# The first block fetch placed ahead of the third chunk's transposes, and a separate tile for VectorE's discarded squares

## The chip, the cores and the metric

The kernel runs on one core of a Trainium2 chip. Five engines take part: TensorE (PE; its weight loads are listed as PEld), VectorE (DVE), ScalarE (ACT), GpSimd (POOL) and SyncE (SP, which here only issues DMAs). The metric is device time of one execution in microseconds, the median over repeated runs.

## What is computed

The input x has 8 sequences of 3584 tokens with 192 features, so 28672 tokens. A causal filter of 7 taps comes first, one set of taps for each of 8 groups of 24 features; each token of the result then goes to one of 8 experts. Cut to what matters:

```python
w = softmax(weight, axis=-1)                       # 8 heads x 7 taps
x = einsum('hk,bskhg->bshg', w, windows_of(x_pad)) # causal filter
xn = x / (norm(x) + 1e-6);  en = emb / (norm(emb) + 1e-6)
logits = xn @ en.T / tau
e = argmax(logits);  gate = softmax(logits)[e]
out = gate * (relu(x @ w1[e]) @ w2[e])             # 192 -> 1024 -> 192
```

## The kernel before

The tokens are handled in 16 **chunks** of 1792 (112 partitions x 16 columns). Matrix products run on pairs of fp16 values, a rounded part and a remainder, so each weight and each token row exists twice.

**The start.** `run()` first loads and prepares the weights of the 8 experts, e = 0 to 7, through three staging buffers. `prep_weights` sums squares on PE (L318) and takes the diagonal of that sum on DVE (L323, whose full result `w_dg` is thrown away and only its row sum kept); ACT then writes the rounded halves (L337, three instructions an expert) and DVE the remainders (L341, three an expert). Between these steps `dispatch` hands out steps of the chunks: `mix` (filter on PE L413, copy on ACT L418, squares of the 16 columns, 12 on ACT L425 and 4 on DVE L428, all of whose full results go to a tile `sq` and are thrown away) and `route` (scaling L457, cast L459, remainder L461 and L464 into `rows`, logits L496, softmax and rank up to L570, which writes `di`, the place of each token in its expert's list; then POOL scatters the rows to `rows_d` in memory, L601). The first two chunks are transposed by PE; from the third on, 16 transposing DMAs a chunk (`turn`, L597) do it, issued by SP.

**Blocks.** Once two chunks are counted, `hand_out` calls `select` (L632), about 25 small DVE instructions in tiles named `sl_*`, each with one buffer in the pool `lone`. They end with two casts (L676, L677) that write `sel`: expert and starting row of each block. The first hand-out makes 7 blocks of 256 tokens. `fetch` (L711) has SP read `sel`, then issue a transposing load `e_xT` (L721) and a small load `e_mt` (L724), which wait for the scatters of the two chunks. `expert` copies the expert's weights to `slot` (L703, L706) and runs a block: 40 matmuls `h_ps` (L776), relu on ACT and DVE (L780, L782), 48 matmuls `o_ps` (L799), gate on ACT (L804), scatter of results by POOL (L806). Blocks and the later chunks' steps are then interleaved to the end of the program.

**What sets the order.** SP runs in the order of the program text. The other engines' instructions are put in an order by a scheduler that works on estimated times and on which tile is free; once placed, each engine runs its list in order. A tile of a pool with one buffer can be handed out again only when its last user is done, so two users of one tag keep the order of the program text between them. `PRE` is (14, 8): after the weights, 14 steps of the chunks, then 8, then the interleaved loop. Before, the hand-out and three fetches stand after the first of the two rounds:

Of the kernel before, what the change touches and what calls it, by code (L numbers as in the profile page):

```python
# [13 lines left out]
F32 = mybir.dt.float32  # L14
# [11 lines left out]
D = 192  # L26
# [3 lines left out]
TP = 112  # L30
# [37 lines left out]
def _dep(tc, frm, to, sync=True):  # L68
    cls = mybir.DependencyClass.Sync if sync else mybir.DependencyClass.NoSync
    tc.add_manual_dep(  # L70
        frm, to, mybir.DependencyInfo(cls, mybir.DependencyReason.DATA),
        reason="routed rows are written before they are read",
    )


class _Moe:
# [217 lines left out]
    def prep_weights(self, e, st):  # L294
        nc = self.nc
        img = self.res[:, e * RES:(e + 1) * RES]


        st, sw = st
        sr, sv = (v.bitcast(BF16).rearrange("p (n k) -> p n k", k=2)[:, :, 1]  # L300
                  for v in (st, sw))
        acc = self.sp.tile([128, 2], F32, tag="w_acc", name="w_acc")
        for k, cols in enumerate(
                ([(sr, 128, i) for i in range(NFC)]
                 + [(sr, 64, i) for i in range(NFC, 2 * NFC)],
                 [(sv, 128, i) for i in range(NFC * D // 128)])):
            if k and e >= BEHIND:

                i = nc.scalar.activation(
                    out=img[:, W2:W2 + NFC * D], in_=sw, func=AF.Square,  # L310
                    accum_out=acc[:, k:k + 1]).ins
                _dep(self.tc, i, self.act[1].name, False)
                yield
                continue
            tr = self.ps("h", [128, 128], F32, "tr_ps")
            for n, (v, rows, i) in enumerate(cols):
                v = v[0:rows, i * 128:(i + 1) * 128]
                i = nc.tensor.matmul(out=tr, lhsT=v, rhs=v, start=(n == 0),  # L318
                                     stop=(n == len(cols) - 1)).ins
                if e >= BEHIND:  # L320
                    _dep(self.tc, i, self.turned.name, False)
            dg = self.sp.tile([128, D], F32, tag="sq", name="w_dg")[:, 0:128]
            nc.vector.scalar_tensor_tensor(  # L323
                out=dg, in0=tr, scalar=1.0, in1=self.idf, op0=ALU.mult,
                op1=ALU.mult, accum_out=acc[:, k:k + 1])
            yield
        ps = self.ps("h", [128, 2], F32, "n2_ps")
        nc.tensor.matmul(out=ps, lhsT=self.onef, rhs=acc, start=True, stop=True)
        s, si = self.pow2(ps, [128, 2], 198, "w_p")
        s1, s2 = s[:, 0:1], s[:, 1:2]  # L330
        nc.vector.tensor_tensor(out=img[:, WS:WS + 2].bitcast(F32), in0=si[:, 0:1],
                                in1=si[:, 1:2], op=ALU.mult)
        yield
        xb = img[:, 2 * F:W2]
        b = img[:, W2:WS].rearrange("p (c d) -> p c d", d=2 * D)
        s_b = sw.rearrange("p (c d) -> p c d", d=D)
        hi = [nc.scalar.activation(out=o, in_=i, func=AF.Copy, scale=m).ins  # L337
              for o, i, m in ((img[:, 0:F], st[:, 0:F], s1),
                              (xb[0:64, :], st[0:64, F:2 * F], s1[0:64]),
                              (b[:, :, 0:D], s_b, s2))]  # L340
        lo = [nc.vector.scalar_tensor_tensor(  # L341
            out=o, in0=i, scalar=m, in1=h, op0=ALU.mult, op1=ALU.subtract).ins
              for o, i, m, h in (
                  (img[:, F:2 * F], st[:, 0:F], s1, img[:, 0:F]),
                  (xb[64:128, :], st[0:64, F:2 * F], s1[0:64], xb[0:64, :]),
                  (b[:, :, D:], s_b, s2, b[:, :, 0:D]))]
        if e >= BEHIND - 1:
            for i in hi:
                _dep(self.tc, i, self.act[e >= BEHIND].name, False)
        for i in lo:  # L350
            if e >= BEHIND - 2:
                _dep(self.tc, i, self.dve[e >= BEHIND].name, False)
            elif e:
                _dep(self.tc, i, self.cut.name, False)
        yield


    def load_x(self, c):
# [46 lines left out]
    def mix(self, c, ring, first):  # L405
        nc, sp = self.nc, self.sp

        yield _Gate(self.asked[c] + LAND_X)
        xt = self.xts[c]
        xc = xt[0:TP]  # L410
        for h in range(H):
            ps = self.ps(ring, [TP, NT, G], F32, "conv_ps")
            i = nc.tensor.matmul(out=ps, lhsT=self.band[:, h, :],  # L413
                                 rhs=xt[:, :, h * G:(h + 1) * G],
                                 start=True, stop=True).ins
            self.behind(i)
            self.clk += STEPC
            nc.scalar.copy(out=xc[:, :, h * G:(h + 1) * G], in_=ps)  # L418
            yield 0.0, 0.46

        n2 = sp.tile([TP, NT], F32, tag="n2", name="n2")
        for t in range(NT):
            sq = sp.tile([128, D], F32, tag="sq", name="sq")[0:TP, :]
            if t % 4 < NACT:
                nc.scalar.activation(out=sq, in_=xc[:, t, :], func=AF.Square,  # L425
                                     accum_out=n2[:, t:t + 1])
            else:
                nc.vector.scalar_tensor_tensor(  # L428
                    out=sq, in0=xc[:, t, :], scalar=1.0, in1=xc[:, t, :],
                    op0=ALU.mult, op1=ALU.mult, accum_out=n2[:, t:t + 1])  # L430
            if t % 2:
                yield ((0.54, 0.0), (0.27, 0.35), (0.0, 0.7))[
                    (t % 4 < NACT) + ((t - 1) % 4 < NACT)]
        s, si = self.pow2(n2[:], [TP, NT], 195, "x_p")
        y = self.rsqrt(n2[:], [TP, NT], "x_r")
        f = sp.tile([TP, NT], F32, tag="f", name="f")
        nc.vector.tensor_tensor(out=f, in0=n2, in1=y, op=ALU.mult)
        nc.vector.scalar_tensor_tensor(out=f, in0=f, scalar=1e-6, in1=s,
                                       op0=ALU.add, op1=ALU.mult)
        nc.vector.reciprocal(out=f, in_=f)  # L440
        nc.vector.tensor_scalar(out=f, in0=f, scalar1=self.rtau[:, 0:1],
                                scalar2=None, op0=ALU.mult)

        yield 1.5, 0.0
        self.mixed[c] = xc, s, si, f
# [460 lines left out]
    def run(self):  # L906
# [15 lines left out]
        first = min(PICK)  # L922
        a, spent = self.dispatch(first, "h"), [0.0, 0.0]
        for e in range(E):
# [9 lines left out]
            if e == BEHIND - 1:  # L934
                for _ in a:
                    pass
                a = self.dispatch(first, "r")
        self.weights_in = True
        for n in PRE:
            for _ in range(n):  # L940
                spent = [s + t for s, t in zip(spent, next(a))]
            if not self.subs:
                self.hand_out(first)
                while self.ready < min(3, len(self.subs)):
                    self.fetch()
        self.gated = True
        live, due, done, out = next(a, None), [0.0, 0.0], False, 0.0
        while live or self.pend or not done or self.at < len(self.subs):
            if self.at < len(self.subs):
                for v in self.expert():  # L950
                    self.steer(spent)
                    out = min(1.0, out + self.pace)
# [41 lines left out]
```

## Time and profile before

| | |
|---|---|
| median of 3 runs | 1357.72 us (1354.47 to 1360.31) |
| the profiled execution | 1352.22 us |
| its span in the trace | 1350.1 us |
| PE busy | 1188.8 us (88%) |
| DVE, ACT, POOL busy | 835.1, 583.3, 543.7 us |
| chain that ended last, largest shares | issue 25%; POOL `out_dram` L806 7% |

The profiled execution is 2.1 us longer than its span and 5.5 us shorter than the median. The page cuts the span in 40 slices and gives each engine's busy tenths:

```profile
PE   5673789897889998999888999889999999999998
DVE  3967657667776756676676564635445555467475
PEclk9666789999899998999998999989999999999999
```

A slice is 33.8 us; the change lies in slices 2 to 6 (34 to 203 us). In a timeline a row is one run of like instructions: start, time until the last ends, engine, line, what it writes and reads, how many (x8), and in brackets how long the engine was idle before it and which event ended that. "issue" or "remote" there means that the trace shows no event.

### The profile page before, as it was taken

The numbers are of one execution on the slowest core, as the hardware profiler recorded it, in microseconds if no ns is written. First come the engines' busy times: TensorE is split into PE (matmuls) and PEld (weight loads), VectorE is DVE, ScalarE is ACT, GpSimd is POOL, SyncE is SP. The second block draws the span as 40 slices with busy tenths as digits, with TensorE's granted clock in tenths as the row PEclk, the third lists the DMA queues.
The fourth block names the chain that finished last, engine by engine and source line by source line (L and its number), as shares of the span: only waits on it lengthen the run. The fifth ranks groups of instructions, "written<-read, shape, count | busy, mean of one in ns | idle before, by whom it ended". The sixth has DMA issues, their size and how long they took to land. (4 is left out here: it accounts for less than half of the span.)

```text
span 1350.1 us, 28933 instructions
## 1 busy us (share of the span) xinstructions
PE 1188.8 (88%) x10572; PEld 911.7 (68%) x10572; DVE 835.1 (62%) x2207; ACT 583.3 (43%) x1343; POOL 543.7 (40%) x541
## 2 busy tenths in 40 slices
PE   5673789897889998999888999889999999999998
PEld 3542578686776676767556667567777777799787
DVE  3967657667776756676676564635445555467475
ACT  4957344444534544544444533324333333333332
POOL 0064252455444546456445555663222222223232
PEclk9666789999899998999998999989999999999999
DMA  9473534536357444565446344312212121113120
GB/s 262 125 221 91 118 76 105 129 94 132 97 128 147 98 115 106 124 138 130 117 119 145 83 103 84 97 63 57 51 37 52 42 52 43 36 40 66 33 45 22
DMA packets 273950, 129.10 MB, mean 96 GB/s; under 512 B 215774, under 2 KB 264285, under 8 KB 273808
## 3 DMA queue, kind: packets, MB, share of 16 engines
q1 hardware_dynamic: 250000, 80.39, 28.2%
q0 software_dynamic: 23808, 46.87, 11.8%
q8 instruction: 83, 1.36, 0.4%
q14 instruction: 59, 0.48, 0.1%
HBM read 38.35 MB, written 47.53 MB: 64 GB/s over the span
## 5 line engine op out<-in xcount | busy, mean ns | idle before, releaser
L799 PE MATMUL o_ps<-slot,hid 128*128 128x192 f16 x5544 | 516.8, 250 | 68.4 <-issue 39.8
L799 PEld LDWEIGHTS <-hid 128*128 128x128 f16 x5544 | 467.4, 100 | 118.7 <-issue 65.8
L776 PE MATMUL h_ps<-e_xT,slot 128*128 128x256 f16 (+2 forms) x2944 | 502.3, 304 | 13.0 <-issue 8.2
L806 POOL DMA_INDIRECT out_dram<-y,e_mt x231 | 259.2, 1122 | 510.4 <-ACT y L804 464.6
L776 PEld LDWEIGHTS <-slot 128*128 128x128 f16 x3680 | 326.5, 99 | 202.4 <-issue 31.2
L782 DVE SCALAR_TENSOR_TENSOR hid<-h_ps,hid 128x512 f16<-128x512 f32 x462 | 309.6, 687 | 194.5 <-ACT hid L780 152.6
L780 ACT ACTIVATE hid<-h_ps 128x512 f16<-128x512 f32 x462 | 267.1, 598 | 236.3 <-PE h_ps L776 166.1
L601 POOL DMA_INDIRECT rows_d<-rows,di x256 | 266.9, 1042 | 222.6 <-issue 84.0
L804 ACT ACTIVATE y<-o_ps,g 128x192 f32<-128x192 f32 x231 | 95.4, 420 | 337.7 <-PE o_ps L799 260.8
L776 PE MATMUL h_ps<-e_xf,slot 128*128 128x256 f16 (+2 forms) x736 | 211.3, 303 | 2.0 <-issue 2.0
L706 DVE COPY slot<-res 128x3074 f16 x88 | 85.9, 976 | 162.4 <-PE o_ps L799 103.3
L413 PE MATMUL conv_ps<-xt,band 128*112 128x384 f32 x256 | 112.2, 545 | 19.0 <-ACT xt L418 7.9
L418 ACT COPY xt<-conv_ps 112x384 f32<-112x384 f32 x128 | 60.1, 480 | 73.9 <-PE conv_ps L413 54.1
L459 ACT CAST rows<-xt 112x768 f16<-112x768 f32 x64 | 52.9, 830 | 75.7 <-DMA rows_d<-rows,di 35.0
L703 DVE COPY slot<-res 128x3072 f16 x88 | 83.7, 952 | 0.0
L496 PEld LDWEIGHTS <-xT 128*112 128x112 f16 x768 | 58.7, 149 | 33.7 <-DMA xT<-rows 20.8
L496 PE MATMUL lg_ps<-ma,xT 128*112 128x16 f16 x512 | 57.9, 204 | 21.3 <-DMA xT<-rows 19.1
L413 PEld LDWEIGHTS conv_ps<-xt,band 128*112 128x112 f32 x256 | 43.2, 195 | 41.1 <-issue 20.5
L461 DVE TENSOR_TENSOR rows<-xt,rows 112x512 f16<-112x512 f32 x64 | 44.0, 687 | 40.5 <-ACT rows L459 30.9
L425 ACT ACTIVATE sq<-xt 112x192 f32<-112x192 f32 x192 | 67.8, 356 | 2.7 <-DVE sq L428 1.7
L457 DVE TENSOR_TENSOR xt<-xt,x_p_s 112x768 f32<-112x768 f32 x64 | 58.3, 952 | 0.2
L496 PE MATMUL lg_ps<-mb,xT 128*112 128x16 f16 x256 | 47.2, 206 | 1.9 <-ACT xT L492 1.4
(163 smaller groups left out, 528.7 us busy)
## 6 DMA issues: line engine op xcount, KB each, us to landing
xt<-in_dram SPq DMA_DIRECT2D x39, 384.0 KB
xt<-in_dram SPq DMA_DIRECT2D x3, 1440.0 KB
rows_d<-rows,di POOLq DMA_INDIRECT x256
res<-in_dram SPq DMA_DIRECT2D x5, 768.0 KB
out_dram<-y,e_mt POOLq DMA_INDIRECT x231
xT<-rows SPq DMA_TRANSPOSE x224
xt<-in_dram SPq DMA_DIRECT2D x2, 1536.0 KB
hid<-in_dram SPq DMA_DIRECT2D x3, 768.0 KB
```

The source lines that it names most:

```text
L413: i = nc.tensor.matmul(out=ps, lhsT=self.band[:, h, :], rhs=xt[:, :, h * G:(h + 1) * G], start=True, stop=True).ins
L425: nc.scalar.activation(out=sq, in_=xc[:, t, :], func=AF.Square, accum_out=n2[:, t:t + 1])
L496: i = nc.tensor.matmul(out=lg[:, g * GX + a, :], lhsT=xT[:, a, k, :], rhs=self.mb if k == 1 else self.ma, start=(k == 0), stop=(k == 2)).ins
L601: i = self.nc.gpsimd.indirect_dma_start(out=self.rows_d[:, :], out_offset=bass.IndirectOffsetOnAxis(ap=idx, axis=0), in_=src, in_offset=No ...
L703: self.under(nc.vector.tensor_copy(out=self.slot[:, 0:W2], in_=v).ins)
L706: self.nc.vector.tensor_copy(out=self.slot[:, W2:], in_=self.res[:, bass.ds(self.we + W2, RES - W2)])
L776: self.mm = nc.tensor.matmul(out=ps[:, c, :], lhsT=w1(o, b + c), rhs=xk[k], start=(i == 0), stop=(i == 4)).ins
L780: self.step = nc.scalar.activation(out=hh[:, b:b + m, :], in_=ps, func=AF.Relu).ins
L782: self.low = nc.vector.scalar_tensor_tensor(out=hl[:, b:b + m, :], in0=ps, scalar=0.0, in1=hh[:, b:b + m, :], op0=ALU.max, op1=ALU.subtrac ...
L799: self.mm = nc.tensor.matmul(out=o, lhsT=h[:, c, q], rhs=w2[:, c, k:k + D], start=(c + i == 0), stop=(c == NFC - 1 and i == 2)).ins
L804: self.step = nc.scalar.activation(out=y, in_=o, func=AF.Copy, scale=g[:, a:a + 1]).ins
L806: i = nc.gpsimd.indirect_dma_start(out=self.out[:, :], out_offset=bass.IndirectOffsetOnAxis(ap=mt[:, a, 0:1], axis=0), in_=y, in_offset=No ...
```

## The change

Two edits. The first hand-out moves from behind the first 14 steps to ahead of them, and each of the two rounds of `PRE` begins with one fetch, where three fetches stood together; the third fetch then comes from `expert`. The thrown-away results of VectorE (four squares a chunk, and `w_dg`) go to a tile of their own, `waste`, in the one-buffer pool under the tag `sl_ge`, a tag that `select` also uses; ScalarE's squares keep `sq`. Lines below L358 move down by 4, those below L425 by 5.

```diff
@@ prep_weights
-            dg = self.sp.tile([128, D], F32, tag="sq", name="w_dg")[:, 0:128]
+            dg = self.waste(128, 128)
@@ new
+    def waste(self, p, n):
+        return self.lp.tile([128, D], F32, tag="sl_ge", name="waste")[0:p, 0:n]
@@ mix
         for t in range(NT):
-            sq = sp.tile([128, D], F32, tag="sq", name="sq")[0:TP, :]
             if t % 4 < NACT:
+                sq = sp.tile([128, D], F32, tag="sq", name="sq")[0:TP, :]
                 nc.scalar.activation(out=sq, ...)
             else:
                 nc.vector.scalar_tensor_tensor(
-                    out=sq, in0=xc[:, t, :], scalar=1.0, in1=xc[:, t, :],
+                    out=self.waste(TP, D), in0=xc[:, t, :], scalar=1.0,
+                    in1=xc[:, t, :],
@@ run
         self.weights_in = True
+        self.hand_out(first)
         for n in PRE:
+            if self.ready < len(self.subs):
+                self.fetch()
             for _ in range(n):
                 spent = [s + t for s, t in zip(spent, next(a))]
-            if not self.subs:
-                self.hand_out(first)
-                while self.ready < min(3, len(self.subs)):
-                    self.fetch()
         self.gated = True
```

On SP, after the last load of weights (`hid`), before: the 16 turns of the third chunk in two groups of eight (`rows_96`), with the input of the fifth chunk (`xt`) between, then the first fetch.

```order
L289 DMA hid<-in_dram 128x8x192
L597 DMA_TRANSPOSE xT<-rows_96 128x3x112 x8
L366 DMA xt<-in_dram 112x192
L375 DMA xt<-in_dram 128x15x192
L597 DMA_TRANSPOSE xT<-rows_96 128x3x112 x8
L714 TENSOR_LOAD sel_3584_1419
L714 ISA x2
L721 ISA
L721 DMA_TRANSPOSE e_xT<-rows_d 128x3x256
L724 ISA
L724 DMA e_mt<-rows_d 128x2x2
```
After:

```order
L289 DMA hid<-in_dram 128x8x192
L719 TENSOR_LOAD sel_3584_1294
L719 ISA x2
L726 ISA
L726 DMA_TRANSPOSE e_xT<-rows_d 128x3x256
L729 ISA
L729 DMA e_mt<-rows_d 128x2x2
L602 DMA_TRANSPOSE xT<-rows_96 128x3x112 x8
L370 DMA xt<-in_dram 112x192
L379 DMA xt<-in_dram 128x15x192
L602 DMA_TRANSPOSE xT<-rows_96 128x3x112 x8
```
The first fetch's six rows, with its reading of `sel`, now stand ahead of the 16 turns and the load of `xt`; the second fetch stands where the first stood, and the rest of SP's list keeps its order.

On DVE, before, the place where `sel` is written: L341 is the last remainder of expert 5's weights, `n_1070` the squares of the third chunk.

```order
L341 SCALAR_TENSOR_TENSOR res<-res,w_p_s 128x8x192
L683 TENSOR_TENSOR sl_t<-sl_t,sl_av 1x8
L663 TENSOR_REDUCE sl_ro<-sl_df 1x7
L676 CAST sel_3584_1419<-sl_se 1x7
L428 SCALAR_TENSOR_TENSOR sq,n_1070<-xt 112x192
L684 SCALAR_TENSOR_TENSOR start<-sl_t,start 1x8
L664 SCALAR_TENSOR_TENSOR sl_ro<-jf,sl_ro 1x7
L677 CAST sel_3584_1419<-sl_ro 1x7
```
After, with the remainders of expert 7 (`hid` is its staging buffer) and the `sl_ge` memset that opens the part of `select` behind the tag:

```order
L341 SCALAR_TENSOR_TENSOR res<-hid,w_p_s,res 128x1024
L658 MEMSET sl_ge 1x63
L341 SCALAR_TENSOR_TENSOR res<-hid,w_p_s,res 64x1024
L143 SCALAR_TENSOR_TENSOR x_r_t<-x_r_t,n_1070 112x16
L659 TENSOR_TENSOR sl_ge<-sl_a,jf 1x7x8
L341 SCALAR_TENSOR_TENSOR res<-hid,w_p_s,res 128x8x192
```
And ten rows further on, where the casts to `sel` now stand (`n_1224` belongs to the fourth chunk):

```order
L681 CAST sel_3584_1294<-sl_se 1x7
L153 TENSOR_SCALAR x_p_e<-n_1224 112x16
L134 TENSOR_SCALAR x_r_sh<-n_1224 112x16
L145 SCALAR_TENSOR_TENSOR x_r_y<-x_r_t,x_r_y 112x16
L669 SCALAR_TENSOR_TENSOR sl_ro<-jf,sl_ro 1x7
L442 TENSOR_TENSOR f<-n_1070,x_r_y 112x16
L682 CAST sel_3584_1294<-sl_ro 1x7
```
The memset stood at the start of the program before, and `sel` was complete ahead of expert 6's remainders. Now the memset comes behind the third of the four squares of the fourth chunk, and the casts come behind the remainders of experts 6 and 7 and behind the third chunk's scaling and rows.

ScalarE's list changes at the start too: expert 1's three L337 stood behind the first chunk's casts (L459) and now stand ahead of them; those of experts 6 and 7 now stand ahead of the casts of the third and the fourth chunk.

On PE, before, the last logits of the third chunk and the start of block 1:

```order
L496 MATMUL lg_ps<-ma,xT 112x16
L496 LDWEIGHTS xT
L496 MATMUL lg_ps<-mb,xT 112x16
L496 LDWEIGHTS xT
L496 MATMUL lg_ps<-ma,xT 112x16
L776 LDWEIGHTS slot
L776 MATMUL h_ps<-e_xT,slot 128x256
```
After, a place inside block 1's first products:

```order
L781 LDWEIGHTS slot
L781 MATMUL h_ps<-e_xT,slot 128x256
L781 LDWEIGHTS slot
L781 MATMUL h_ps<-e_xT,slot 128x256
L501 LDWEIGHTS xT
L501 MATMUL lg_ps<-ma,xT 112x16
L501 LDWEIGHTS xT
L501 MATMUL lg_ps<-mb,xT 112x16
L501 LDWEIGHTS xT
L501 MATMUL lg_ps<-ma,xT 112x16
L781 LDWEIGHTS slot
```
Before, all 48 logits of the third chunk precede block 1. Now they are spread between its products, in groups of three to nine, and the last stand behind most of block 1 and ahead of block 2.

## Rows read from the trace of the kernel before

**Rows 1.** Busy us (instructions) by stretch: PE, PEld, DVE, ACT, POOL; granted clock; DMA; GB/s

```profile
125.00:150.00 25.00, 10.43 (x55) 7.36 (x56) 20.31 (x54) 12.22 (x24) 0.00 (x0) 0.50 0.52 116
150.00:175.00 25.00, 17.95 (x162) 14.88 (x161) 14.95 (x60) 5.93 (x11) 10.07 (x10) 0.84 0.53 114
900.00:1100.00 200.00, 195.94 (x1744) 145.54 (x1744) 96.22 (x164) 71.70 (x138) 54.90 (x54) 0.98 0.22 49
```

**Rows 2.** PE groups, 85 to 250 us: busy, mean ns | idle before, releasers

```profile
L799 PE MATMUL o_ps<-slot,hid 128*128 128x192 f16 x401 | 40.7, 257 | 9.8 <-issue 7.0 <-DVE hid L782 2.4 <-DVE slot L706 0.3
...
L496 PE MATMUL lg_ps<-ma,xT 128*112 128x16 f16 x72 | 9.9, 216 | 16.8 <-DMA xT<-rows 16.8
```

**Rows 3.** PE timeline: start, duration, work xcount [idle before <-releaser]

```profile
122.62 0.26 PE L496 MATMUL lg_ps<-ma,xT 128*112 128x16 f16 x1 [9.52 <-DMA xT<-rows]
...
149.11 3.31 PE L776 MATMUL h_ps<-e_xT,slot 128*128 128x256 f16 x16 [2.51 <-DMA e_xT<-rows_d]
...
158.89 0.82 PE L776 MATMUL h_ps<-e_xT,slot 128*128 128x256 f16 x6
...
163.25 2.33 PE L799 MATMUL o_ps<-slot,hid 128*128 128x192 f16 x24
...
177.08 1.06 PE L776 MATMUL h_ps<-e_xT,slot 128*128 128x256 f16 x4
```

**Rows 4.** Timeline of SP's DMA queue: start, time to issue, transfer

```profile
120.09 11.18 SPq L597 DMA_TRANSPOSE xT<-rows  x8
...
132.49 12.07 SPq L597 DMA_TRANSPOSE xT<-rows  x8
146.06 1.23 SPq L721 DMA_TRANSPOSE e_xT<-rows_d  x1
...
148.70 1.24 SPq L721 DMA_TRANSPOSE e_xT<-rows_d  x1
...
153.34 10.88 SPq L597 DMA_TRANSPOSE xT<-rows  x8
```

**Rows 5.** DVE timeline, from the second chunk's `di` to the last weights

```profile
93.14 0.15 DVE L570 TENSOR_SCALAR di<-dr 112x16 int32<-112x16 f32 x1
...
93.50 1.28 DVE L341 SCALAR_TENSOR_TENSOR res<-hid,w_p_s,res 128x1024 f16<-128x1024 f32 x1
...
96.41 1.80 DVE L341 SCALAR_TENSOR_TENSOR res<-hid,w_p_s,res 128x1536 f16<-128x1536 f32 x1
...
103.42 0.34 DVE L428 SCALAR_TENSOR_TENSOR sq<-xt 112x192 f32<-112x192 f32 x1
...
103.96 0.16 DVE L677 CAST sel<-sl_ro 1x7 int32<-1x7 f32 x1
...
118.79 0.29 DVE L323 SCALAR_TENSOR_TENSOR w_dg<-tr_ps,idf 128x128 f32<-128x128 f32 x1 [3.36 <-remote]
...
129.46 2.69 DVE L457 TENSOR_TENSOR xt<-xt,x_p_s 112x768 f32<-112x768 f32 x3
...
133.09 0.68 DVE L461 TENSOR_TENSOR rows<-xt,rows 112x512 f16<-112x512 f32 x1
133.69 0.42 DVE L464 TENSOR_TENSOR rows<-xt,rows 112x256 f16<-112x256 f32 x1
...
140.51 1.81 DVE L341 SCALAR_TENSOR_TENSOR res<-hid,w_p_s,res 128x1536 f16<-128x1536 f32 x1
```

**Rows 6.** ACT timeline: expert 1's weights, the second chunk's casts, a `relu`

```profile
43.26 3.65 ACT L337 ACTIVATE res<-hid,w_p_s 128x1024 f16<-128x1024 f32 x3
...
52.24 2.65 ACT L459 CAST rows<-xt 112x768 f16<-112x768 f32 x3 [0.83 <-DVE xt L457]
...
169.78 0.60 ACT L780 ACTIVATE hid<-h_ps 128x512 f16<-128x512 f32 x1 [5.51 <-remote]
```

**Rows 7.** Waits of the whole run: who <- whom: us, times, longest

```profile
DVE sq L428 <- ACT sq L425: 28.8, 22, 6.3
```

**Rows 8.** POOL timeline: the last scatter of the second chunk

```profile
116.78 0.94 POOL L601 DMA_INDIRECT rows_d<-rows,di  x1 [0.30 <-issue]
```

## The prediction

> **What bounds the kernel now.** I first read the busy shares by stretch [rows 1]. From 900 to 1100 us TensorE is busy 195.94 of 200 us: there the blocks run back to back, so whatever moves the point at which they start moves the end by as much, and a wait of another engine costs nothing. In the 25 us from 125 on, TensorE is busy 10.43, with the granted clock at 0.50, the lower of its two levels (1.2 of 2.4 GHz), and in the next 25 us 17.95. The change has to be priced in that start.
>
> Next, what TensorE waits for there [rows 2]. Between 85 and 250 us it waits 16.8 us for transposed rows (`xT`) of the third chunk ahead of its logits, and 7.0 us inside blocks for no event that the trace shows. The timeline [rows 3] gives the places: logits start at 122.62 after 9.52 us idle, block 1's first products at 149.11 after 2.51 us for its `e_xT`, block 2's at 158.89, block 3's only at 177.08, because between 163.25 and 177 block 2's second products trickle out while ScalarE too sits idle 5.51 us with no event named [rows 6].
>
> Then the queue that feeds it [rows 4]. SP issues eight turns from 120.09, which take 11.18 us, eight more from 132.49 (12.07 us), and only then the first fetch, at 146.06, with the second at 148.70. The fetch could have gone far earlier: `sel` is written at 103.96 [rows 5] and the last scatter it needs is issued at 116.78 [rows 8]. So the fetch is late by its place in SP's list, and that place is what the first edit changes.
>
> **The change part by part.** *The fetch's new place.* No instruction is added; six rows of SP's list move ahead of 16 turns and an input load. If `sel` were still written at 103.96, the fetch would start by about 119, some 27 us earlier, and the turns would lose only its 2.6 us. But everything on SP behind the fetch now waits for `sel`, and by the order `sel` is written much later. So the question is when.
>
> *When `sel` is written.* The thrown-away squares now share the tag of `sl_ge`, so the memset that opens the second half of `select` stands behind the third square of the fourth chunk, and with it behind nearly all of VectorE's remaining start. From `di` of the second chunk, at 93.14, to the last cast at 103.96+0.16 it was 11.0 us, of which six L341 took 8.7 (four of 1.28, two of 1.80), one square 0.34, and some 21 small instructions the other 1.9, 0.09 each [rows 5]. By the order of the changed kernel there stand between the two points: 12 L341 (8x1.28 + 4x1.80 = 17.4), four scalings (2.69/3 each, 3.6), four pairs of L461 and L464 (0.68+0.42 each, 4.4), eight squares (2.7), two `w_dg` (0.6) and about 47 small ones (4.2). That is 32.9 us. One `w_dg` waited 3.36 us before [rows 5], and stands in this stretch now: 36.3.
>
> `di` itself comes later. ScalarE now does expert 1's three L337, 3.65 us, ahead of the first chunk's casts; ScalarE's idle time ahead of the second chunk's casts, 0.83, takes up a part [rows 6]. So 93.14+2.8 = 95.9, with 0 and 3.65 as the ends. `sel` then comes at 95.9+36.3 = **132.2**, 28 us later than before. With no wait and no delay of `di` it would be 126.0.
>
> *From `sel` to block 2.* SP's chain behind `sel` is: reading it, 1.5 us (from the end of the second eight turns, 132.49+12.07, to 146.06); one fetch, 148.70-146.06 = 2.6; then what stood between the first turn and the first block's products, 149.11-120.09 = 29.0. In that, the turns took 11.18 and 12.07 while rows were still being written; eight with rows at hand took 10.88 [rows 4], so I take 1.5 off: 27.5. Together 31.6 (33.1 with nothing taken off). At the end of this chain stands the second fetch, so block 2, not block 1, starts at 132.2+31.6 = 163.8. It started at 158.89 [rows 3]: **+4.9 us**. The point at which the edit pays nothing is `sel` at 127.3.
>
> Block 1's own products can start about 12 us earlier than 149.11 (132.2+1.5, and the 3.05 that lie between 146.06 and 149.11). That gain doesn't reach the end. TensorE's list puts the third chunk's logits between block 1's products, and these wait for turns that start about 16 us later than before, at 136.3. Block 1 is what hides the turns now, but the turns outlast it by far (96 products, 149.11 to 158.89 in all).
>
> A page bears on this against the change. The Trainium skill (Perfetto Trace Analysis, section "DMA Instruction — HWDGE (DVE, Sync)") shows a DMA's semaphore wait standing in the sequencer, ahead of the issue and ahead of the time that a profile reports. By that rule the turns stand still while the fetch waits, as the sum above has it; would a waiting fetch let them pass, they would start at 120 as before and the +4.9 would be nothing. The trace of before agrees as far as it goes: the fetch shows no row until the turns ahead of it have gone at 144.56, with `sel` ready 42 us before its start [rows 4, 5].
>
> *The tile for squares.* VectorE no longer waits for ScalarE to give up a `sq` buffer: 28.8 us over the run in 22 waits [rows 7]. Most of that lies where TensorE is the full engine [rows 1] and is worth nothing there; in the start it may be worth 1 us, with 0 and 3 as ends. ScalarE's squares keep two buffers and lose a sharer, no cost.
>
> *TensorE's clock.* Block 1's first 16 products took 3.31 us, 0.21 each, in the stretch at the lower level; block 2's first six took 0.82, 0.14 each [rows 3]. If the waits for turns now lie just ahead of block 2, it pays up to 16x0.07 = 1.1. I take 0.6.
>
> *The idle 7.0 us in block 2* [rows 2] has no named cause; I leave it in the forecast, and its going is a rival.
>
> Sum: 4.9 + 0.6 - 1.0 = **+4.5 us** on 1352.22, so 1356.7 for an execution like the profiled one; that one lay 5.5 below the median of 1357.72, which gives **1362.2**. By the ends (`sel` 128 to 134, the clock 0 to 1.1, squares 0 to -3) about 1357 to 1366.
>
> **The rivals.** *The fetch really comes early (faster).* The order on VectorE costs less than I priced: `sel` near 127.3 or before, which needs the 3.36 us wait gone and `di` little delayed, so that block 2 starts no later; and weights that are finished earlier (their last L341 now stands ahead of `sel`, before it ran until 142.3 [rows 5]) and a calmer queue take the unexplained 7.0 us out of block 2. Then -1.0-7.0 = -8: 1349.7; with `sel` at 124, -11: 1346. For it: the start is bound by a chain of waits and TensorE is mostly idle in it [rows 1]. Against: nothing shows that the 7.0 us belong to the queue or the weights. The Trainium skill (DMA: Bandwidth & Descriptors, section "Rules for kernel authors") advises to issue a DMA early, compute, and wait for it late. By that rule this rival would be the rule; but the fetch is early in the list alone, since its address is computed late.
>
> *VectorE's new chain is longer (slower).* Expert 7's whole preparation now stands ahead of `sel`. If its `w_dg` also waits 3.36, and ScalarE's L337 of 3.65 [rows 5, 6] comes in series with the L341 that read it, `sel` is 7.0 later, at 139.2: +11.5, so 1369.2. It decides once `sel` is later than about 134.4, where the sum passes 0.5%. For it: on every engine of the start the waits are in series. Against: VectorE has other work to lay beside them, if the order has put it there.
>
> *The two cancel (no change).* Block 2 starts about 5 us later, and that falls into the 7.0 us that TensorE waited anyway, since what was late there has more time: 1357.7.
>
> **How the numbers follow.** Forecast +4.5: 0.52; faster rival 0.20; slower rival 0.17; cancelling 0.11. A measurement here can tell about 0.5%, 6.8 us, so the bounds are 1350.9 and 1364.5. Of the forecast 0.36 lies within and 0.16 above; of the faster rival 0.18 below and 0.02 within; of the slower 0.16 above and 0.01 within; of the cancelling 0.09 within and 0.02 below. Faster 0.20, same 0.48, slower 0.32. The range runs from 1347, near the faster rival's far end, to 1371, just over the slower one; the forecast's own is 1357 to 1366.
>
> **What would show it.** In the changed trace: the second cast to `sel` at about 132 (before 127 speaks for the faster rival, after 134 for the slower one); the first fetch 1.5 us behind it and the first turn of the third chunk directly behind the fetch, near 136; block 1's products near 137, broken up by logits that wait for `xT`; block 2 at about 164; VectorE's waits for ScalarE's `sq` gone. If the turns start near 120 with `sel` still unwritten, SP's list isn't what holds them and the main term is wrong; if block 3 follows block 2 without the idle 7 us, the cancelling or the faster case has come.

## The result: slower by 0.9%

The changed kernel takes 1367.58 us (median of 17 runs, 1360.16 to 1375.41), the kernel before 1354.47 us beside it (17 runs); the ratio is 1.0087, with a 95% interval of 1.0068 to 1.0106. By that ratio it is +11.8 us (9.2 to 14.4); the two medians are 13.1 us apart. The forecast was 1362.2 with +4.5 us, inside 1347 to 1371; the likeliest case was a change too small to measure. The direction was right and the size 2.6 times too small. The experiments put the larger part in the start, in a chain that the sum had not followed, and the rest in the later chunks.

### The profile after

The busy times by stretch, as in [rows 1] (PE, PEld, DVE, ACT, POOL, granted clock, DMA share, GB/s), with the next stretch added:

```profile
125.00:150.00 25.00, 13.90 (x112) 11.29 (x112) 19.65 (x60) 7.13 (x14) 2.20 (x2) 0.67 0.40 99
150.00:175.00 25.00, 20.65 (x159) 16.34 (x160) 12.41 (x45) 6.20 (x13) 3.09 (x4) 0.80 0.48 90
175.00:200.00 25.00, 12.01 (x69) 7.63 (x67) 4.01 (x7) 3.00 (x7) 15.39 (x16) 0.66 0.39 94
```
and before, the last of these stretches:

```profile
175.00:200.00 25.00, 24.88 (x212) 20.76 (x211) 12.36 (x30) 13.09 (x43) 13.89 (x13) 0.91 0.24 63
```
TensorE does 6.2 us more than before from 125 to 175, and then loses half of the stretch from 175 to 200, in which it was full before: 12.01 us busy, not 24.88. The change brings work forward, and something behind takes more than that away.

VectorE's timeline, as in [rows 5]: the second chunk's `di`, expert 7's discarded sum, the last cast to `sel`.

```profile
93.86 0.15 DVE L575 TENSOR_SCALAR di<-dr 112x16 int32<-112x16 f32 x1
...
107.50 0.29 DVE L323 SCALAR_TENSOR_TENSOR waste<-tr_ps,idf 128x128 f32<-128x128 f32 x1 [1.04 <-PE tr_ps L318]
...
127.91 0.15 DVE L682 CAST sel<-sl_ro 1x7 int32<-1x7 f32 x1
```
`sel` is complete at 128.06, against 104.12. `di` is 0.7 us later, not 2.8, and the wait at the discarded sum of expert 7 is 1.04, not 3.36. SP's queue, as in [rows 4]:

```profile
129.30 1.34 SPq L726 DMA_TRANSPOSE e_xT<-rows_d  x1
...
131.40 11.83 SPq L602 DMA_TRANSPOSE xT<-rows  x8
```
The first fetch goes 1.24 us behind `sel`, and the third chunk's turns directly behind the fetch, at 131.40 and not at 120.09. Between the last load of weights and the fetch no row of this queue stands, as the forecast had it. What SP waited for is its reading of `sel` ahead of the fetch, which starts at 128.1. The Trainium skill (Perfetto Trace Analysis, section "DMA Instruction — HWDGE (DVE, Sync)") describes the like for a DMA's own semaphore wait: it stands in the sequencer, ahead of the time that a profile reports. TensorE's timeline, as in [rows 3]:

```profile
132.49 3.57 PE L781 MATMUL h_ps<-e_xT,slot 128*128 128x256 f16 x16 [17.63 <-DMA e_xT<-rows_d]
...
159.74 3.57 PE L781 MATMUL h_ps<-e_xT,slot 128*128 128x256 f16 x16 [2.42 <-DMA e_xT<-rows_d]
...
170.83 1.04 PE L781 MATMUL h_ps<-e_xT,slot 128*128 128x256 f16 x8
...
175.20 2.39 PE L804 MATMUL o_ps<-slot,hid 128*128 128x192 f16 x27
...
190.89 0.32 PE L804 MATMUL o_ps<-slot,hid 128*128 128x192 f16 x1 [2.46 <-issue]
191.62 0.32 PE L804 MATMUL o_ps<-slot,hid 128*128 128x192 f16 x1 [0.41 <-issue]
...
193.73 0.65 PE L804 MATMUL o_ps<-slot,hid 128*128 128x192 f16 x3 [0.39 <-issue]
...
197.73 1.06 PE L781 MATMUL h_ps<-e_xT,slot 128*128 128x256 f16 x4
```
Block 1 starts at 132.49 and block 2 at 159.74, only 0.85 us later than before. Block 3 starts at 170.83, 6.3 us **earlier** than before. Then its second products, from 175.20 on, stop: 27 run at full pace, and from 177.6 to 193.7 they come one by one, at multiples of some 0.7 us (190.89, 191.62, 193.73), with "issue" as the only reason. Block 4 starts at 197.73. Before, it was

```profile
189.78 0.60 PE L776 MATMUL h_ps<-e_xT,slot 128*128 128x256 f16 x4
```
so 7.95 us later. In this pair of executions the lag isn't simply carried to the end. Block 12 starts 3.6 us later than before; before:

```profile
283.98 1.47 PE L776 MATMUL h_ps<-e_xT,slot 128*128 128x256 f16 x12
```
after:

```profile
287.56 0.49 PE L781 MATMUL h_ps<-e_xT,slot 128*128 128x256 f16 x3
```
The spans are 1350.1 and 1367.5 us, so the other 13.8 us arise behind block 12. Single executions of one kernel here differ by more than 10 us (before: 1347.28 to 1361.2), so the pair can't divide the loss between the start and the rest; the experiments do.

ScalarE in the stretch from 177 to 194 of the changed kernel:

```profile
181.56 0.60 ACT L785 ACTIVATE hid<-h_ps 128x512 f16<-128x512 f32 x1 [6.08 <-remote]
```
GpSimd's timeline of the changed kernel, the first scatter of the third chunk and the last of the row:

```profile
171.65 1.39 POOL L606 DMA_INDIRECT rows_d<-rows,di  x1 [21.30 <-issue]
...
190.04 0.94 POOL L606 DMA_INDIRECT rows_d<-rows,di  x1 [0.30 <-issue]
```
and GpSimd before:

```profile
160.07 1.12 POOL L601 DMA_INDIRECT rows_d<-rows,di  x1 [36.09 <-ACT y L804]
...
171.61 1.26 POOL L601 DMA_INDIRECT rows_d<-rows,di  x1 [0.30 <-issue]
```
Before, TensorE stood still from 165.6 to about 175 and ScalarE for 5.51 us [rows 2, 3, 6]; the third chunk's scatters ran from 160.07 to 172.87. After, the standstill is from 177.6 to 193.7, and the scatters run from 171.65 to 190.98. Both times it begins 5 to 6 us behind the first scatter and ends 2 to 3 us behind the last of the row, which is GpSimd with 0.30 us between one and the next. Before, the row held ten of GpSimd's indirect DMAs (eight scatters and two of results), after, fifteen (thirteen and two). That is a lead, not a proof; the last group of experiments tests it. Not every row does it. Before, GpSimd issued seven indirect DMAs in a row from 177.06 on:

```profile
177.06 1.35 POOL L806 DMA_INDIRECT out_dram<-y,e_mt  x1 [4.19 <-ACT y L804]
...
185.59 0.94 POOL L601 DMA_INDIRECT rows_d<-rows,di  x1 [0.30 <-issue]
```
and TensorE stayed busy through it, as the stretch from 175 to 200 above shows.

Some waits of the whole run (who waits for whom: us, times, longest), after:

```profile
ACT rows L464 <- DMA rows_d<-rows,di: 61.6, 22, 10.6
...
DVE x_p_e L153 <- ACT sq L429: 7.9, 3, 5.4
...
DVE waste L432 <- ACT xt L422: 7.1, 5, 3.3
```
and the first of these before:

```profile
ACT rows L459 <- DMA rows_d<-rows,di: 35.0, 16, 4.1
```
ScalarE's casts wait 26.6 us longer for scatters in all, which fits scatters that come later. VectorE's wait of 28.8 us for ScalarE's buffers [rows 7] is gone by name. It has moved in part: to the copy of the filter's result (7.1) and to the step behind the squares (7.9), which needs all of ScalarE's squares anyway.

### The profile page after: what moved, and what is told of

It is laid out like the page before. It is cut to its first block, busy times and chain, and to the rows that moved or that the text cites. A ratio compares the mean times of both kernels' runs of the same rounds, so it can differ in the third digit from the quotient of the medians.

```text
span 1367.5 us, 28953 instructions
## 1 busy us (share of the span) xinstructions
PE 1198.7 (88%) x10572; PEld 915.1 (67%) x10572; DVE 839.1 (61%) x2207; ACT 578.7 (42%) x1343; POOL 548.0 (40%) x541
## 4 chain that ended last, share of the span: by engine, by line
issue 26%; PE 13%; POOL 8%; DVE 1%; ACT 1%; DMA 1%; POOLq 0%; another core or an unknown queue 0%; SPq 0%; DVEq 0%; ACTq 0%
POOL out_dram L811 8%; PE h_ps L781 6%; PE o_ps L804 6%; PE conv_ps L417 1%; POOL rows_d L606 1%; DVE hid L787 1%; DMA rows_d<-rows,di 0%; PE lg_ps L501 0%; POOLq L811 0%; SPq L602 0%; ACT hid L785 0%; DMA xT<-rows 0%; DVE xt L462 0%; ACT sq L429 0%
## 5 line engine op out<-in xcount | busy, mean ns | idle before, releaser
L781 PE MATMUL h_ps<-e_xT,slot 128*128 128x256 f16 (+2 forms) x2944 | 508.4, 306 | 38.9 <-DMA e_xT<-rows_d 20.1
L811 POOL DMA_INDIRECT out_dram<-y,e_mt x231 | 264.0, 1143 | 537.1 <-ACT y L809 480.2
L711 DVE COPY slot<-res 128x3074 f16 x88 | 86.2, 979 | 166.9 <-PE o_ps L804 107.9
```

Source lines behind the costliest of these rows:

```text
L711: self.nc.vector.tensor_copy(out=self.slot[:, W2:], in_=self.res[:, bass.ds(self.we + W2, RES - W2)])
L781: self.mm = nc.tensor.matmul(out=ps[:, c, :], lhsT=w1(o, b + c), rhs=xk[k], start=(i == 0), stop=(i == 4)).ins
L811: i = nc.gpsimd.indirect_dma_start(out=self.out[:, :], out_offset=bass.IndirectOffsetOnAxis(ap=mt[:, a, 0:1], axis=0), in_=y, in_offset=No ...
```

## The experiments

Each group of kernels was timed on one chip together with the kernel before, and every ratio is against that, with its 95% interval. The chips differ by some 12 us in the kernel before (medians 1343 to 1356), so times of two groups aren't compared, ratios are. A difference in us is worked out from the ratio where nothing else is said. The diffs of the first two groups, and of the first kernel of the third, are against the changed kernel.

### One edit at a time

The first edit alone, with the squares of VectorE in `sq`:

```diff
     def waste(self, p, n):
-        return self.lp.tile([128, D], F32, tag="sl_ge", name="waste")[0:p, 0:n]
+        return self.sp.tile([128, D], F32, tag="sq", name="waste")[0:p, 0:n]
```

> The first edit alone: the hand-out and its first fetch stand ahead of the third chunk's transposes, and VectorE's squares stay in sq. Theory (the changed kernel is late because sel is written behind all of VectorE's start, and the third chunk's turns wait on SP behind the fetch): here sel comes back to about 105, the first fetch goes at about 119 when the second chunk's scatters have landed, the turns start near 122 and block 2 near 152; nothing is slower than before, -7 to 0 us against before. Rival (the early fetch itself costs, by splitting block 1 or by its place on SP): it stays at about +10 us although sel is early.

Measured 0.9986 (0.9971 to 1.0002), -1.9 us. The last cast to `sel` on VectorE:

```profile
104.73 0.16 DVE L682 CAST sel<-sl_ro 1x7 int32<-1x7 f32 x1
```
The SP queue, first fetch and first turns:

```profile
120.14 1.43 SPq L726 DMA_TRANSPOSE e_xT<-rows_d  x1
...
122.34 11.61 SPq L602 DMA_TRANSPOSE xT<-rows  x8
```
`sel` is early again, the fetch goes when the scatters allow it, and the turns lose 2.3 us. Nothing is slower, so an early place of the fetch costs nothing by itself. It brings next to nothing either: TensorE's list had the third chunk's logits ahead of block 1 here, and block 1 started at 149.71.

The second edit alone:

```diff
         self.weights_in = True
-        self.hand_out(first)
         for n in PRE:
-            if self.ready < len(self.subs):
-                self.fetch()
             for _ in range(n):
                 spent = [s + t for s, t in zip(spent, next(a))]
+            if not self.subs:
+                self.hand_out(first)
+                while self.ready < min(3, len(self.subs)):
+                    self.fetch()
```

> The second edit alone: VectorE's discarded squares in the tile with the tag sl_ge, the hand-out and the three fetches where they stood before. Theory (sel late costs only where turns stand behind it): sel is late, about 127, but the turns start near 120 as before and the first fetch at about 146 finds sel ready: 0 +-3 us against before. Rival (the shared tag costs by itself, since it holds VectorE's list): +5 to +12 us.

Measured 1.0073 (1.0047 to 1.0098): the expectation of no cost was wrong. Its profiled execution took 1354.13, 9.5 us below its median, so its trace isn't read for the cause; the next group looks for it.

Both edits, with a tag of its own for the squares:

```diff
-        return self.lp.tile([128, D], F32, tag="sl_ge", name="waste")[0:p, 0:n]
+        return self.lp.tile([128, D], BF16, tag="waste", name="waste")[0:p, 0:n]
```

> Both edits, but the discarded squares have a tag of their own in the one-buffer pool (16-bit, so that the memory suffices). Theory (the shared tag holds sel, and with it SP): sel near 105 to 112, turns near 122, as with the first edit alone: -7 to 0 us against before. Rival (the fetch's place is the cost): about +10 us.

Measured 1.0023 (1.0002 to 1.0044), +3.1 us: between the two. `sel` was at 105.7 again. So most of the changed kernel's loss goes with the shared tag, but not all. One part of the expectation fell: the turns didn't start near 122.

```profile
129.21 11.34 SPq L602 DMA_TRANSPOSE xT<-rows  x8
```
Here they waited for the third chunk's rows, whose first remainder VectorE made at 128.12, not at 119.01 as before. The standstill that follows the late turns was as long as in the changed kernel (about 173 to 188), yet block 4 started at 191.78, against 190.9 with the first edit alone, since block 3 had started 12 us earlier than there. A long standstill is thus no loss by itself; it depends on what stands ahead of it.

### Where the second edit costs

To part the start from the rest, `waste` was used for some chunks only, `sq` for the others; `c` is the chunk, and `w_dg` counts as chunk 0.

```diff
-    def waste(self, p, n):
-        return self.lp.tile([128, D], F32, tag="sl_ge", name="waste")[0:p, 0:n]
+    def waste(self, p, n, c=0):
+        if c < 4:                      # c >= 4 in the other half
+            return self.lp.tile([128, D], F32, tag="sl_ge", name="waste")[0:p, 0:n]
+        return self.sp.tile([128, D], F32, tag="sq", name="sq")[0:p, 0:n]
```

The second edit alone, in the start only, in the later chunks only, and everywhere with a tag of its own:

> The second edit alone and only in the start: w_dg and the squares of the first four chunks in the tile with the tag sl_ge, the later chunks' in sq as before. Theory (the cost of the second edit lies behind the start, where later hand-outs meet the squares): 0 +-3 us against before. Rival (it lies in the start, where sel comes at 130): +6 to +10 us.

> The other half: w_dg and the first four chunks' squares in sq as before, from the fifth chunk on in the tile with the tag sl_ge. Theory (the cost lies behind the start): +6 to +10 us against before, with a mean granted clock lower by about 0.005. Rival (it lies in the start): 0 +-3 us.

> The second edit alone (hand-out where it stood before), but with a tag of its own and 16-bit. Theory (the tie between the squares and select through the shared tag costs): no tie, so 0 +-3 us against before. Rival (taking VectorE's squares out of sq is itself the cost, as it changes the order on VectorE and ScalarE): +6 to +10 us, as with the shared tag, which measured +8.

Measured: start only 1.0006 (0.9972 to 1.0040), later chunks only 1.0035 (1.0003 to 1.0067), own tag everywhere 1.0045 (1.0009 to 1.0080). With the start only, `sel` is nearly as late as in the changed kernel (VectorE's timeline):

```profile
126.57 0.16 DVE L684 CAST sel<-sl_ro 1x7 int32<-1x7 f32 x1
```
And the SP queue, first turns and first fetch:

```profile
116.66 11.23 SPq L604 DMA_TRANSPOSE xT<-rows  x8
...
142.73 1.23 SPq L728 DMA_TRANSPOSE e_xT<-rows_d  x1
```
but `sel` comes before the turns have gone, and nobody waits. A late `sel` is free where the fetch stands behind the turns. In the later chunks the edit costs some 0.4%, with intervals that reach almost down to nothing, and the tie through the tag isn't needed for it, since a tag of its own (16-bit, and in the start too) cost as much. That theory fell. The two halves together come to 0.4%, less than the 0.73% of the second edit alone, though the intervals meet.

Then the changed kernel with the second edit in the start only, `sel` late and the turns behind it:

> The changed kernel, with the second edit only in the start (w_dg and the first four chunks): sel is late, and the third chunk's turns stand behind it on SP. Theory (the changed kernel's +11.8 is about +8 from the later chunks' squares and +4 from the start): +2 to +6 us against before. Rival (it is the start with its longer standstill alone): +9 us or more.

Measured 1.0074 (1.0044 to 1.0104), +10 us, far above the 2 to 6 expected (the medians are 8.9 us apart; the profiled execution is the lowest of its twelve, 5.1 us below their median). Its SP queue repeats the changed kernel's:

```profile
129.46 1.33 SPq L728 DMA_TRANSPOSE e_xT<-rows_d  x1
...
131.56 11.51 SPq L604 DMA_TRANSPOSE xT<-rows  x8
```
and so do blocks 2, 3 and 4 on TensorE:

```profile
159.82 3.57 PE L783 MATMUL h_ps<-e_xT,slot 128*128 128x256 f16 x16 [2.54 <-DMA e_xT<-rows_d]
...
170.25 1.04 PE L783 MATMUL h_ps<-e_xT,slot 128*128 128x256 f16 x8
...
195.66 1.06 PE L783 MATMUL h_ps<-e_xT,slot 128*128 128x256 f16 x4
```
Four kernels make a square for the start, with the squares of the later chunks as before in all: both as before 0; `sel` late alone 0 (1.0006); fetch early alone -1.9 us (0.9986); both +10 us (1.0074). Neither half costs anything; together they do. Of the four only the last has SP hold the turns back for `sel`. It is also the only one in which TensorE's list has the third chunk's logits inside block 1, and no run parts the two.

### The standstill

The scatters of the third chunk, spread out: eight tiny memsets on GpSimd behind each. Each memset is ordered behind the one before it, the next scatter behind the last.

```diff
     def put(self, step=None):
         ...
         self.scatter(idx, src)
+        if c == 2:
+            self.space()
...
+    def space(self):
+        g = self.lp.tile([128, 32], F32, tag="gap", name="gap")
+        last = self.scatters[-1]
+        for _ in range(8):
+            i = self.nc.gpsimd.memset(g, 0.0).ins
+            _dep(self.tc, i, last.name, False)
+            last = i
+        self.gap = last
```

> The changed kernel with eight tiny memsets on GpSimd behind each scatter of the third chunk, so that these scatters no longer follow each other without a break. In the changed kernel all engines step about once in 0.7 us from 177 to 194, towards the end of 15 scatters in a row; before it was 165 to 175, in a row of 10. Theory (the row of scatters causes the standstill): it shrinks by at least 8 us and the time comes down to 0 to +4 us against before. Rival (the standstill comes from the transposes, or from program loading at this place): it stays, +10 us or more.

Measured 1.0097 (1.0074 to 1.0121): no gain. But the trace says something else than the rival. TensorE, the start of block 4 and a wait two blocks later:

```profile
183.09 0.60 PE L795 MATMUL h_ps<-e_xT,slot 128*128 128x256 f16 x4
...
222.60 0.98 PE L818 MATMUL o_ps<-slot,hid 128*128 128x192 f16 x5 [8.38 <-ACT hid L799]
```
ScalarE just ahead of that wait's end:

```profile
221.22 0.83 ACT L465 CAST rows<-xt 112x768 f16<-112x768 f32 x1 [10.80 <-DMA rows_d<-rows,di]
```
Block 4 starts at 183.09, not at 197.73: the standstill is gone. Most of these 14.6 us is lost again in one place: ScalarE's cast of the fifth chunk waits 10.80 us for the scatters of the third, whose `rows` buffer it overwrites (there are two), and the relu that TensorE needs stands behind that cast on ScalarE; TensorE waits 8.38. The spread scatters ended too late.

So the pause came shorter: 16 memsets behind every fourth scatter.

```diff
+        if c == 2 and len(self.scatters) % 4 == 0:
+            self.space()          # with 16 memsets
```

> The changed kernel with a pause of 16 tiny memsets (about 2.8 us) on GpSimd behind every fourth scatter of the third chunk. The scatters in a row are four to five then, and the last comes about 9 us later at most, not 30 as with a pause behind each. Theory (a row of more than some five scatters holds up all engines): no stretch near 177 to 194 in which engines step in 0.7 us; block 4 starts near 183 to 187, not at 197.7, and the time comes to 0 to +7 us against before. Rival (the standstill is not the scatters'): block 4 near 197 and +10 us or more.

> The kernel before with the same pauses in the third chunk's scatters. Theory: the 7.0 us of standstill in block 2 go, block 3 starts near 170, not at 177; -7 to 0 us against before (a part may be given back where ScalarE's casts of the fifth chunk wait for the scatters). Rival: block 3 at 177, 0 to +4 us.

> The first edit alone (sel early, squares in sq) with the same pauses. If the early hand-out and the pauses both do what they are for, -9 to -2 us against before; if the pauses do nothing, -2 us, as with the first edit alone.

Measured: changed kernel with pauses 1.0045 (1.0018 to 1.0072), the kernel before with pauses **0.9950** (0.9921 to 0.9980), the first edit with pauses 0.9964 (0.9934 to 0.9994). The changed kernel with pauses, on TensorE:

```profile
180.67 0.42 PE L818 MATMUL o_ps<-slot,hid 128*128 128x192 f16 x3 [1.99 <-issue]
...
184.08 0.60 PE L795 MATMUL h_ps<-e_xT,slot 128*128 128x256 f16 x4
...
219.94 0.50 PE L818 MATMUL o_ps<-slot,hid 128*128 128x192 f16 x2 [8.12 <-ACT hid L799]
```
and on ScalarE:

```profile
218.24 0.83 ACT L465 CAST rows<-xt 112x768 f16<-112x768 f32 x1 [11.26 <-DMA rows_d<-rows,di]
```
Some 2 us of the standstill are left (block 4 at 184.08), half of the loss against the kernel before is back, and the cast waits 11.26 us for scatters again, TensorE 8.12. (The profiled execution, 1358.85, is the slowest of its twelve, so its rows show where the time goes and not how much.)

But the pauses do as much for the kernel before. The two kernels with pauses, on the same chip, are 1349.21 and 1337.25 us, 0.9% apart, as without pauses. So the standstill as such isn't what parts them: with most of it taken out of both, the change costs as much as ever. In their traces the two are level up to block 6 (207.28 and 207.54), and block 7, behind the cast's wait, starts at 226.38 with the change and at 215.87 without. What the change does is to make the third chunk's scatters late. Without pauses that shows as a longer standstill, with them as this wait, which the kernel before with pauses doesn't have (its longest wait of this kind up to 230 us is 1.8). The first edit alone with pauses, 1340.63, has `sel` early and lies 3.4 us from the kernel before with pauses, within the intervals.

The kernel before with pauses, blocks 2 and 3:

```profile
159.74 0.82 PE L790 MATMUL h_ps<-e_xT,slot 128*128 128x256 f16 x6
...
173.52 0.83 PE L790 MATMUL h_ps<-e_xT,slot 128*128 128x256 f16 x4
```
Block 3 comes 13.8 us behind block 2, before 18.2 [rows 3]; the idle time that no event ends in block 2 is 1.5 us. The instructions of TensorE and of ScalarE stand in the same order in both, so most of the unexplained 7.0 us of the kernel before [rows 2] belonged to the row of scatters as well.

Last, the kernel before with the pauses in the first three chunks (`c <= 2`):

> The kernel before with the pauses behind every fourth scatter of the first three chunks, not the third alone. If rows of scatters hold up the engines in the start too (67 to 118 us, 16 in a row twice), VectorE's and TensorE's unexplained waits of 3 to 7 us there shrink and the time is 0.5 to 1.2% below before, better than the 0.5% of the third chunk alone; the first fetch isn't delayed, since it goes at 146 and the scatters end by about 135. Rival (the start is held by other waits): as with the third chunk alone, 0.995, or worse where the fourth chunk's casts wait for the second's scatters.

Measured **0.9914** (0.9880 to 0.9948), the fastest of all. Blocks 1 and 3:

```profile
141.97 3.57 PE L790 MATMUL h_ps<-e_xT,slot 128*128 128x256 f16 x16 [3.62 <-DMA e_xT<-rows_d]
...
163.04 0.60 PE L790 MATMUL h_ps<-e_xT,slot 128*128 128x256 f16 x4
```
Block 1 starts 7.1 us earlier than before, and block 3 14.0 us earlier [rows 3], 10.1 us behind block 2. VectorE's waits between 60 and 130 us, with the pauses:

```profile
DVE rows L462 <- ACT rows L460: 5.1, 1, 5.1
```
and before:

```profile
DVE w_dg L323 <- remote: 7.1, 2, 3.8
...
DVE w_p_e L153 <- remote: 3.1, 1, 3.1
```
The "remote" waits, 10.2 us in three, are no longer there (the wait in [rows 5] at 118.79 was one of them). One wait for ScalarE, 5.1 us, is new; all of VectorE's waits in this stretch together come to about 15 us, before to 21. So rows of scatters held up the start of the kernel before as well.

## Why the prediction was right in direction and short in size

- **The direction is partly luck.** The forecast rested on block 2, 4.9 us late. It was 0.85 us late, so that the sum's main term came to next to nothing, and the loss arose elsewhere. The slower rival's time, 1369.2, lies nearest to the measured one, but what it needed, `sel` later than forecast, didn't happen.
- **`sel` late, and SP's turns behind it: right.** Forecast 132.2, measured 128.06. `di` was over-priced by 2.1 us and a wait by 2.3. The square of four kernels shows that this pair is what costs in the start.
- **From `sel` to block 2, 31.6 us: right.** Measured 159.74-128.06 = 31.7. The difference between +0.85 and +4.9 is thus the error in `sel` alone. (A block has 88 products, not the 96 of the prediction; no term hangs on it.)
- **TensorE's clock, 0.6 us: too small.** Block 2's first 16 products took 3.57 us, and its 40 products 7.1 (159.74 to 166.9), not 4.4 as before: +2.8.
- **The squares, -1.0 us: wrong sign.** Outside the start they cost about +0.4%, 4.7 to 6 us (1.0035, and 1.0045 with a tag of their own everywhere). VectorE's waits changed their place rather than going; which of the orders that the scheduler then chose costs the time, the runs don't settle.
- **The idle 7.0 us left as they were: wrong.** I took an unexplained stretch as a constant. Most of it belongs to the third chunk's row of scatters, and these come behind that chunk's turns, logits and ranks. With the turns 11.3 us later, the row came against more of block work, was longer (fifteen, not ten, without a break) and stood on block 3: from 6.3 us ahead at block 3 to 7.95 behind at block 4.
- **The chain was followed to block 2 and no further: the step that failed.** The turns lead not only to block 2 but to the third chunk's scatters, and these free the buffer of the fifth chunk's casts. The changed kernel with pauses shows that this second end is there, at some 8 us, once most of the standstill is out of the way, and that the change then costs 0.9% all the same. I asked who waits for the fetch, and not what else the turns feed.
- **The faster rival** had the weights finished earlier and a calmer queue take the 7.0 us away. Most of them can be taken out, but by what GpSimd does; with `sel` early and the turns near 122 (the first edit alone) TensorE still lost 7.0 us there, and block 3 started at 178.0. **The cancelling rival**, a later block 2 falling into the old standstill, happened in its first half: block 2 +0.85 and block 3 -6.3.

The sum as measured: the start with both edits 1.0074, the squares of the later chunks 1.0035, together 1.011, beside the 1.0087 (1.0068 to 1.0106) of the whole. Each part's interval is about 0.6% wide, so this fits and doesn't prove the division.

## What to carry to other kernels

An early place in an in-order queue is early only if its operand is: look up where the address of a moved transfer is computed, and count what stands behind it. Two edits that each cost nothing in a stretch can cost there together, so an edit that delays a value and an edit that makes a queue wait for it have to be priced as a pair. An idle stretch without a named cause isn't a constant: find what it runs along with, here a row of indirect DMAs, before assuming that it stays, and follow a delayed step to every end that it feeds.

## What the runs showed of the hardware

In the two rows of indirect DMAs that GpSimd issued for the third chunk with 0.30 us between them (ten before, fifteen after), the other engines slowed to one instruction per 0.7 us or multiples of it, from 5 to 6 us behind the row's first until 2 to 3 us behind its last, with no event that the trace names. TensorE lost 7.0 us so before; ScalarE and VectorE stood for 5 to 6 us at a time. Pauses of about 3 us behind every fourth scatter took most of it away (block 3 13.8 and not 18.2 us behind block 2) and, in three chunks, 0.9% of the time of the kernel before. A row of seven from 177.06 to 186.53 before had no such effect on TensorE, and how long a row has to be, or what else it takes, the runs don't show. Nor do they show what is shared there: DMA engines were busy for a mean share of 0.39 from 175 to 200 in the changed kernel, less than the 0.48 of the stretch ahead of it, in which TensorE was busy 20.65 of 25 us, so it isn't their mean load.
